# Rows of the first down projection by two engines, urgent splits of v, and two banks of scores in one visit

## The chip, the cores and the metric

The kernel runs on one core of a Trainium2 chip. The metric is the device time of one execution in microseconds (us). The time before the change is the median of three runs. One execution was also taken with the hardware profiler; that is the one whose rows are shown.

## The reference

Sliding-window attention with a distance bias feeds a bilinear feed-forward network (FFN). There are 8 batches, 8 heads, 576 positions, a head dimension of 64; the FFN has 512 inputs, 1536 hidden units and 512 outputs. All is float32.

```python
scores = q @ k.T / sqrt(64) + slopes[h] * (-|i - j|)    # only 0 <= i - j < 128, else -1e9
attn   = softmax(scores)
x      = (attn @ v) laid out as [4608 tokens, 512]
out    = ((x @ w_a) * (x @ w_b)) @ w_out
```

## The kernel before

Every float32 operand of a large product is split into two float16 parts, high and low, after scaling by a power of two, and a product is three matmuls (high-high, high-low, low-high). So most elementwise work is of the form "ACT makes the high part, DVE subtracts it for the low part".

**Attention** goes by pairs of heads, four pairs p = 0 to 3 in a batch. Four PSUM tiles (banks 0 to 3 of `BANKS`) hold a pair's scores. `scores(o, bi)` does the matmuls of one bank (L361 in batch 1, L365 later), then for each of its tiles a bias with minimum on DVE (L369) and an exponential with sum on ACT (L370). `normalize` scales the finished tiles and splits them into `phl` (ACT L382, DVE L383). `transpose_probs` transposes `phl` by DMA into `pT` (L388). `split_v` splits a pair's `v` into `vhl` (ACT L282, DVE L283), with a scale `st.sv` that `v_scale` makes from sums of squares (PE `vtot` L272, then DVE L107, L113, L114). `pv` multiplies `pT` with `vhl` into two PSUM tiles `x_ps` (L482), ACT evicts them into x, in the space of `v`, and takes x's square (`square_x`, L407), which POOL adds to `xq` (L409). After pair 3, `split_x` splits x into `xs` for the FFN, and `hidden_scale` sums the squares over partitions on PE (`n_ps`, L496) and makes the FFN's scale `st.g`. q and k are loaded (SP, L298, L299), split (`split_qk`: ACT L325, DVE L326) and laid out by four DMAs (`qst`, `qkh`, `qkl`, L334 to L337) before a pair's first scores.

**The FFN** of a batch is an up projection (`up_ps`, or `p` and `ch`, L805) and a down projection (`dn_ps`: L787 in batch 0, L901 later). The hidden tiles `rc` come from `new_hidden()`, three buffers; `row()` has two buffers. `bank()` hands out five PSUM tiles in turn for the FFN; three others, of the pool `ps_at`, serve scores, `x_ps` and sums.

**The order.** Batch 0's attention (`first_attention`) comes first, by itself, while the FFN's weights are loaded and converted (generators `up_weights`, `down_weights`: ACT L130, DVE L131 and L133, POOL L135, ACT L141; at the end DVE L222 and the split of the down weights, ACT L230 and DVE L231). Then the FFN of batch b is interleaved with the attention of the batches after it: `attention()` is a generator with places i, one a pair, in sevenths, and `att.along` steps it beside the FFN's groups. A `yield` ends a visit: what stands between two yields goes to TensorE between two pieces of FFN work. In batch 1 and later PE's order is the order of the program; the order of ACT, DVE and POOL, and in batch 0 PE's too, is made by a planner from modelled times and from each instruction's priority, which is its place in the program. SP's order is that of the program up to the end of batch 0's FFN. `tc.high_priority(offset=PRIO)` puts instructions ahead of all that is ready without it. Each engine then takes its instructions strictly in that order. The evictions of the later up and down projections are urgent in this way; those of batch 0's down projection and the splits of `v` are not.

The first down projection, `first_down`, makes four PSUM rows (e = 0 to 3) for each half of the tokens (t = 0, 1) at once, f outermost; ACT writes each to a `row()` buffer (L791) and issues its transfer (L792).

From attention batch 4 on (`two == 2`), banks 0 and 1 of a pair's scores are already done in one visit, and banks 2 and 3 in two visits.

Of the kernel before, what the change touches and what calls it, by code (L numbers as in the profile page):

```python
# [13 lines left out]
BF16 = mybir.dt.bfloat16  # L14
# [3 lines left out]
AF = mybir.ActivationFunctionType  # L18
ALU = mybir.AluOpType
AX = mybir.AxisListType.X  # L20

B, H, S, D = 8, 8, 576, 64
DM, DF = 512, 1536
P = 128
NPAIR = H // 2
# [3 lines left out]
HT = S // 2  # L29
# [13 lines left out]
PRIO = 2000  # L43
# [3 lines left out]
def attention_then_bilinear_ffn(ctx: ExitStack, tc: tile.TileContext, qT, kT, vP, w_a, w_b, w_out, rel, slopes2, outT):  # L47
    nc = tc.nc
    vec, act, pe, pool, sp = nc.vector, nc.scalar, nc.tensor, nc.gpsimd, nc.sync
# [229 lines left out]
    def split_v(st, p):  # L279

        vhl = work.tile([P, 2, VCOLS], F16, tag="vhl", name="vhl", bufs=2)
        act.activation(vhl[:, 0, :], st.v[:, p, :], AF.Copy, scale=st.sv)  # L282
        vec.scalar_tensor_tensor(out=vhl[:, 1, :], in0=st.v[:, p, :], scalar=st.sv, in1=vhl[:, 0, :], op0=ALU.mult, op1=ALU.subtract)  # L283
        return vhl

    def load_plain_qk(b, p):
# [87 lines left out]
    def normalize(o):  # L374

        a, z = o.parts[0][0], o.n

        vec.tensor_scalar(out=o.rin[:, a:z], in0=o.sm[:, a:z], scalar1=1e-9, scalar2=1.0 / PSC, op0=ALU.add, op1=ALU.mult)
        vec.reciprocal(o.rin[:, a:z], o.rin[:, a:z])
        for m, e, pc, w in o.parts:  # L380
            s = o.rin[:, m:m + 1]
            act.activation(phl[:, 0, pc:pc + w], e, AF.Copy, scale=s)  # L382
            vec.scalar_tensor_tensor(out=phl[:, 1, pc:pc + w], in0=e, scalar=s, in1=phl[:, 0, pc:pc + w], op0=ALU.mult, op1=ALU.subtract)  # L383
        o.parts = []
# [12 lines left out]
            act.activation(x[:, c:c + w], ps[:, 0:w], AF.Copy, scale=scale)  # L397
        square_x(p, st, x)

    def square_x(p, st, x, add=True):  # L400

        if p == 0:
            act.activation(st.xq, x, AF.Square, scale=1.02)
            st.squares = [st.xq]
        else:
            sq = work.tile([P, S], BF16, tag="sq", name="sq")
            act.activation(sq, x, AF.Square, scale=1.02)  # L407
            if add:
                pool.tensor_tensor(out=st.xq, in0=st.xq, in1=sq, op=ALU.add)  # L409
            else:  # L410
                st.squares.append(sq)

    B12 = 7

# [69 lines left out]
    def pv(p, st, o, vhl):  # L484
        xp = new_x_ps()
        hi, lo = o.pT[:, 0:NCOL // P, :], o.pT[:, NCOL // P:2 * NCOL // P, :]
        each_pv(xp, (vhl[:, 0, :], vhl[:, 1, :], vhl[:, 0, :]), (hi, hi, lo))
        keep_x(p, st, xp, 1.0 / PSC)
# [16 lines left out]
    def first_attention(weights, rate):  # L505
# [12 lines left out]
        for p in range(NPAIR):  # L518
# [4 lines left out]
            if p == 0:  # L523
# [3 lines left out]
                st = load_v(0)  # L527
# [52 lines left out]
        def pv(p, pt):  # L580


            rin = small.tile([P, QT], F32, tag="rin", name="rin0")
            vec.tensor_scalar(out=rin, in0=sums[p], scalar1=1e-9, scalar2=None, op0=ALU.add)
            vec.reciprocal(rin, rin)
            yield
            rp = [ps_ch.tile([P, 512], F32, tag="ch", name="rin_ps") for _ in range(2)]
            for i in range(QT):
                for e in range(2):
                    r = slice(64 * e, 64 * e + 64)  # L590
                    pe.matmul(rp[i // 8][r, 64 * (i % 8):64 * (i % 8) + 64], rin[r, i:i + 1].to_broadcast([64, 64]), ident[r, r], start=True, stop=True)
            r = first.tile([P, S], F32, tag="rin0", name="rin0", bufs=1)
            x = st.v[:, p, 0:S]
            for n, (c, w) in enumerate(halves_of_x):
                act.copy(r[:, c:c + w], rp[n][:, 0:w])
            xp = [ps_ch.tile([P, 512], F32, tag="ch", name="x_ps") for _ in range(2)]
            each_pv(xp, (st.v[:, p, :],), (pt,))
            yield
            for n, (c, w) in enumerate(halves_of_x):
                vec.scalar_tensor_tensor(out=x[:, c:c + w], in0=xp[n][:, 0:w], scalar=st.sv, in1=r[:, c:c + w], op0=ALU.mult, op1=ALU.mult)  # L600
            yield
            square_x(p, st, x, p < NPAIR - 1)
            yield

        bias(0)
# [33 lines left out]
    def attention():  # L639


        n = NPAIR * (B - 1)
        qks = {}

        def load(i):
            if i < n:

                qks[i] = (load_plain_qk if i < NPAIR else load_qk)(1 + i // NPAIR, i % NPAIR)

        def squares(i):  # L650
            if i >= n:
                return None
            qk = qks.pop(i)
            return qk if i < NPAIR else qk_squares(1 + i // NPAIR, i % NPAIR, qk)

        def split(o):
            if o and o.b > 1:
                split_qk(o)

        def lay_out(o):  # L660
            if o:
                before_scores(o, lay_out_qk(o) if o.b > 1 else -8.0)

        def behind():

            return tc.issue_after(last_read[0].ins) if last_read[0] else ExitStack()

        load(0)
        st, prev = load_v(1), None
        o = squares(0)  # L670
        lay_out(o)
        load(1)
        yield 0
        for i in range(n + 1):
            b, p = 1 + i // NPAIR, i % NPAIR

            two = 2 if o and o.b >= 4 else 1
            for bi in range(two if o else 0):
                scores(o, bi)
            with behind():  # L680
                nxt = squares(i + 1)
            if p == 1 and b > 1:
                st = load_v(b)
            if p == 2:
                v_scale(st)
            yield i + 1 / 7
            if o and two == 1:
                scores(o, 1)

            if p == 2:  # L690

                with tc.issue_after(first_reads[0].ins) if first_reads[0] else ExitStack():
                    late.vhl = split_v(st, late.p)
            elif prev and p != 1:
                prev.vhl = split_v(st, prev.p)
            yield i + 2 / 7
            if p == 2:
                pv(late.p, st, late, late.vhl)
                transpose_probs(prev)
                split(nxt)  # L700
            if o and p != 2:
                with behind():
                    normalize(o)
            if p != 2:
                split(nxt)
            yield i + 3 / 7
            if o:
                scores(o, 2)
            if prev and p not in (1, 2):
                pv(prev.p, st, prev, prev.vhl)  # L710
            yield i + 4 / 7
            if p == 2:
                prev.vhl = split_v(st, prev.p)
                with behind():
                    normalize(o)
            if o:
                scores(o, 3)
            lay_out(nxt)
            load(i + 2)
            if p == 1:  # L720
                v_squares(st, (0, 1))
            if prev and p == 0:
                states[b - 1] = st
                assert started["down"] == b - 2
                for k, _ in enumerate(split_x(st, b - 1 <= 2, b - 1 >= 2)):
                    yield i + (4.2 + 0.2 * k) / 7
            yield i + 5 / 7
            if o:
                with behind():
                    normalize(o)  # L730
            if p == 1:
                v_squares(st, (2, 3))
            yield i + 6 / 7
            if prev and p == 0:
                hidden_scale(st)
            if p == 2:
                pv(prev.p, st, prev, prev.vhl)
            if p == 1:
                late = prev
            elif o:  # L740
                transpose_probs(o)
            prev, o = o, nxt
            yield i + 1
# [4 lines left out]
    def new_hidden():  # L748
        return work.tile([P, 2, HT], F32, tag="rc", name="rc", bufs=3)
# [29 lines left out]
    def first_down(b, oi, h):  # L779

        started["down"] = b
        for t in range(2):
            pss = [bank("dn_ps") for _ in range(NE)]
            for f in range(NF):
                for e in range(NE):
                    for n, (wi, hi) in enumerate(((0, 0), (0, 1), (1, 0))):
                        pe.matmul(pss[e][:, 0:HT], wdn[:, f, wi, e * P:(e + 1) * P], h[:, f, t, hi, :], start=(f == 0 and n == 0), stop=(f == NF - 1 and n == 2))  # L787
                yield
            for e in range(NE):
                o = row()  # L790
                act.activation(o, pss[e][:, 0:HT], AF.Copy, scale=oi)  # L791
                act.dma_start(outT[e * P:(e + 1) * P, b * S + t * HT:b * S + (t + 1) * HT], o)  # L792

    def row():
        return work.tile([P, HT], F32, tag="row", name="row", bufs=2)
# [234 lines left out]
```

## Time and profile before

| | |
|---|---|
| median of three runs | 1038.46 us (1038.11 to 1038.9) |
| the profiled execution | 1035.06 us, its span 1033.3 us |
| granted TensorE clock, mean | 0.98 |
| PE busy | 980.7 us, 95% of the span |
| DVE, ACT, POOL busy | 677.4, 647.5, 315.6 us |

Times in rows are microseconds from the span's start. A row of the order of time has start, duration, engine, line, operation, tiles (out<-in), shapes and count; brackets at its end tell how long the engine was idle before it and what ended that. PE is the matmuls, PEld the weight loads, SPq and ACTq the sequencers that issue transfers. A row of the stretches has the stretch, its length and the busy time of each engine with its count of instructions, then granted clock, share of the DMA engines, GB/s. A row of the transfers has the number issued, KB each, and us from issue to landing. Rough places: batch 0's attention ends at 66, its up projection at 170, its down projection at 219; the FFN of batch 1 begins there; from 570 on each FFN batch takes some 113 us, and the last ends the span.

### The profile page before, as it was taken

The numbers are of one execution on the slowest core, as the hardware profiler recorded it, in microseconds if no ns is written. First come the engines' busy times: TensorE is split into PE (matmuls) and PEld (weight loads), VectorE is DVE, ScalarE is ACT, GpSimd is POOL, SyncE is SP. The second block draws the span as 40 slices with busy tenths as digits, with TensorE's granted clock in tenths as the row PEclk, the third lists the DMA queues.
The fourth block names the chain that finished last, engine by engine and source line by source line (L and its number), as shares of the span: only waits on it lengthen the run. The fifth ranks groups of instructions, "written<-read, shape, count | busy, mean of one in ns | idle before, by whom it ended". The sixth has DMA issues, their size and how long they took to land.

```text
span 1033.3 us, 23882 instructions
## 1 busy us (share of the span) xinstructions
PE 980.7 (95%) x9325; PEld 754.8 (73%) x9325; DVE 677.4 (66%) x1880; ACT 647.5 (63%) x1672; POOL 315.6 (31%) x348
## 2 busy tenths in 40 slices
PE   8789979889999899889999999999999999999998
PEld 6556657667777677667777777777777778787776
DVE  5889988355778656985767667765776576534430
ACT  7977778556667756667666676667666765423321
POOL 3544562000368205880222212321223012221100
PEclk8899989999999999999999999999999999999999
DMA  8335733462543532435434743453624732200001
GB/s 344 125 111 195 251 86 73 100 155 58 123 88 86 145 74 56 87 80 153 88 65 86 184 90 65 88 116 115 124 52 99 173 65 42 48 31 11 1 13 35
DMA packets 148433, 102.83 MB, mean 100 GB/s; under 512 B 120032, under 2 KB 128352, under 8 KB 147296
## 3 DMA queue, kind: packets, MB, share of 16 engines
q1 hardware_dynamic: 138816, 91.77, 35.8%
q10 hardware_dynamic: 9504, 9.54, 2.9%
q8 instruction: 73, 1.20, 0.5%
q14 instruction: 40, 0.33, 0.1%
HBM read 48.33 MB, written 9.44 MB: 56 GB/s over the span
## 4 chain that ended last, share of the span: by engine, by line
PE 58%; DVE 15%; DMA 12%; ACT 7%; issue 3%; POOL 3%; SPq 2%; ACTq 0%; DVEq 0%; POOLq 0%
PE ch L805 16%; PE p L805 13%; PE dn_ps L901 11%; PE up_ps L805 10%; PE x_ps L482 4%; DMA pT<-phl 3%; DVE phl L383 3%; PE sc_ps L365 2%; DVE t L369 2%; ACT phl L382 1%; DMA v<-in_vP 1%; DMA qk<-in_kT 1%; DMA qst<-qkl 1%; DMA qst<-qkh 1%; DMA qkl<-qkl 1%
## 5 line engine op out<-in xcount | busy, mean ns | idle before, releaser
L805 PEld LDWEIGHTS <-wup 128*128 128x128 f16 x4212 | 407.7, 98 | 126.9 <-issue 18.6
L901 PE MATMUL dn_ps<-h,wdn 128*128 128x288 f16 x2016 | 256.8, 287 | 2.5 <-DVE h L799 2.5
L805 PE MATMUL ch<-xs,wup 128*128 128x288 f16 x1584 | 230.0, 287 | 6.7 <-DVE rc L865 4.3
L901 PEld LDWEIGHTS <-wdn 128*128 128x128 f16 x2016 | 193.9, 98 | 56.6 <-issue 3.7
L805 PE MATMUL up_ps<-xs,wup 128*128 128x288 f16 x1440 | 188.1, 289 | 6.0 <-ACT row L791 3.7
L805 PE MATMUL p<-xs,wup 128*128 128x288 f16 x1188 | 178.7, 287 | 0.0
L860 POOL TENSOR_TENSOR rc<-rc,row 128x288 f32<-128x288 f32 x66 | 64.5, 978 | 254.0 <-DVE row L858 235.6
L370 ACT ACTIVATE t<-t,mn 128x192 f32<-128x192 f32 (+2 forms) x252 | 107.4, 428 | 38.6 <-DVE mn L369 36.9
L383 DVE SCALAR_TENSOR_TENSOR phl<-t,rin,phl 128x192 f16<-128x192 f32 (+2 forms) x252 | 103.9, 447 | 34.5 <-ACT phl L382 34.5
L798 ACT CAST h<-rc 128x576 f16<-128x576 f32 x96 | 64.3, 669 | 64.0 <-DVE rc L865 33.1
L382 ACT ACTIVATE phl<-t,rin 128x192 f16<-128x192 f32 (+2 forms) x252 | 88.6, 426 | 19.4 <-DMA pT<-phl 11.4
L799 DVE TENSOR_TENSOR h<-rc,h 128x576 f16<-128x576 f32 x90 | 72.2, 802 | 26.4 <-ACT h L798 25.9
L369 DVE CUSTOM_DVE_ANT_0 t<-sc_ps,bias,neg 128x192 f32<-128x192 f32 (+2 forms) x216 | 74.3, 389 | 13.4 <-PE sc_ps L365 9.6
L842 ACT ACTIVATE row<-ch,g 128x288 f32<-128x288 f32 x66 | 32.9, 498 | 66.0 <-PE ch L805 66.0
L417 DVE TENSOR_TENSOR xs<-v,xs 128x576 f16<-128x576 f32 x51 | 52.5, 1044 | 28.4 <-ACT xs L416 27.9
L135 POOL TENSOR_TENSOR wup<-wup,wdn 128x512 int32<-128x512 int32 x36 | 56.9, 1602 | 33.7 <-issue 5.6
L906 ACT ACTIVATE row<-dn_ps,oi 128x288 f32<-128x288 f32 x56 | 27.7, 495 | 60.4 <-PE dn_ps L901 60.4
L837 DVE TENSOR_TENSOR rc<-p,rc 128x288 f32<-128x288 f32 x66 | 30.0, 454 | 45.5 <-PE p L805 41.5
L409 POOL TENSOR_TENSOR xq<-xq,sq 128x576 bf16<-128x576 bf16 x23 | 34.1, 1481 | 83.7 <-ACT sq L407 83.3
L482 PE MATMUL x_ps<-pT,vhl 128*64 128x128 f16 (+3 forms) x1176 | 47.8, 233 | 5.4 <-DVE vhl L283 2.6
L482 PEld LDWEIGHTS <-vhl 128*64 128x64 f16 (+1 forms) x1176 | 44.1, 112 | 11.2 <-issue 3.9
L365 PEld LDWEIGHTS <-qst 128*64 128x64 f16 x864 | 30.8, 110 | 27.8 <-issue 24.6
(139 smaller groups left out, 1301.1 us busy)
## 6 DMA issues: line engine op xcount, KB each, us to landing
v<-in_vP SPq DMA_DIRECT2D x8, 1280.0 KB, 6.6
out<-row ACTq DMA_DIRECT2D x64, 144.0 KB, 1.8
qk<-in_qT SPq DMA_DIRECT2D x28, 288.0 KB, 3.9
qk<-in_kT SPq DMA_DIRECT2D x28, 288.0 KB, 4.4
wdn<-in_w_a SPq DMA_DIRECT2D x12, 512.0 KB, 4.0
wdn<-in_w_b SPq DMA_DIRECT2D x12, 512.0 KB, 4.9
wdn<-in_w_out SPq DMA_DIRECT2D x12, 512.0 KB, 4.8
qst<-qkh SPq DMA_DIRECT2D x24, 144.0 KB, 2.4
```

The costliest lines, as they stand in the source:

```text
L135: pool.tensor_tensor(out=t[:, m, :], in0=t[:, m, :], in1=low[:, m, :], op=ALU.add)
L369: vec.tensor_tensor_reduce(out=t[:, c:c + w], in0=ps[:, c:c + w], in1=o.bias[:, WIN - w:WIN], scale=-0.125 if o.b == 1 else o.neg, scalar= ...
L370: act.activation(t[:, c:c + w], t[:, c:c + w], AF.Exp, bias=o.mn[:, n:n + 1], scale=-1.0, accum_out=o.sm[:, n:n + 1])
L382: act.activation(phl[:, 0, pc:pc + w], e, AF.Copy, scale=s)
L383: vec.scalar_tensor_tensor(out=phl[:, 1, pc:pc + w], in0=e, scalar=s, in1=phl[:, 0, pc:pc + w], op0=ALU.mult, op1=ALU.subtract)
L417: vec.tensor_tensor(out=xs[:, n, 1, :, :], in0=src, in1=xs[:, n, 0, :, :], op=ALU.subtract)
L482: pe.matmul(xp[oc // 512][64 * h:64 * h + 64, o0:o0 + w], vt[0:rows, c:c + 64], probs(pt, rows, blocks, h), start=(n == 0 and first), stop ...
L798: act.copy(h[:, f, :, 0, :], hid)
L799: eng.tensor_tensor(out=h[:, f, :, 1, :], in0=hid, in1=h[:, f, :, 0, :], op=ALU.subtract)
L805: pe.matmul(ps[:, 0:HT], wup[:, a[0], a[1], wi, k, :], xs[:, b, xi, k, :], start=(first and n == 0), stop=(last and n == len(ks) - 1), ski ...
L860: pool.tensor_tensor(out=x0, in0=x0, in1=mid, op=ALU.mult)
L901: pe.matmul(ps[:, 0:HT], wdn[:, f, wi, e * P:(e + 1) * P], h[:, f, t, hi, :], start=(m == 0 and n == 0), stop=(m == NF - 1 and n == 2))
```

## The change

Four edits.

- `split_v`: its two instructions are urgent until batch 1's x is complete (`states.get(1)`), that is for the four pairs of batch 1.
- `square_x` in batch 0: the square of pair 2 is kept in a tile of its own in the pool `first`, as pair 3's already was in `work`, and goes to `hidden_scale` as one more operand of the sum on PE. Only pair 1's is added by POOL.
- `attention()`: from batch 4 on, for pairs 1 and 3, `scores(o, 3)` follows `scores(o, 2)` (and pair 3's `pv`) in the same visit. Pairs 0 and 2 stay.
- `first_down`: rows 0 and 2 by ACT, 1 and 3 by DVE, all urgent; rows 2 and 3 are written to a tile of `new_hidden()`, not to `row()`. ACT still issues their transfers.

```diff
     def split_v(st, p):
         vhl = work.tile([P, 2, VCOLS], F16, tag="vhl", name="vhl", bufs=2)
-        act.activation(vhl[:, 0, :], st.v[:, p, :], AF.Copy, scale=st.sv)
-        vec.scalar_tensor_tensor(out=vhl[:, 1, :], in0=st.v[:, p, :], scalar=st.sv, in1=vhl[:, 0, :], op0=ALU.mult, op1=ALU.subtract)
+        with tc.high_priority(offset=PRIO) if not states.get(1) else ExitStack():
+          act.activation(vhl[:, 0, :], st.v[:, p, :], AF.Copy, scale=st.sv)
+          vec.scalar_tensor_tensor(out=vhl[:, 1, :], in0=st.v[:, p, :], scalar=st.sv, in1=vhl[:, 0, :], op0=ALU.mult, op1=ALU.subtract)
         return vhl
...
-    def square_x(p, st, x, add=True):
+    def square_x(p, st, x, keep=None):
         if p == 0:
             act.activation(st.xq, x, AF.Square, scale=1.02)
             st.squares = [st.xq]
+        elif keep:
+            sq = keep.tile([P, S], BF16, tag="sq", name="sq")
+            act.activation(sq, x, AF.Square, scale=1.02)
+            st.squares.append(sq)
         else:
             sq = work.tile([P, S], BF16, tag="sq", name="sq")
             act.activation(sq, x, AF.Square, scale=1.02)
-            if add:
-                pool.tensor_tensor(out=st.xq, in0=st.xq, in1=sq, op=ALU.add)
-            else:
-                st.squares.append(sq)
+            pool.tensor_tensor(out=st.xq, in0=st.xq, in1=sq, op=ALU.add)
...
-            square_x(p, st, x, p < NPAIR - 1)
+            square_x(p, st, x, first if p == 2 else work if p == 3 else None)
...
             if prev and p not in (1, 2):
                 pv(prev.p, st, prev, prev.vhl)
+            if two == 2 and p in (1, 3):
+                if p == 2:
+                    with behind():
+                        normalize(o)
+                scores(o, 3)
             yield i + 4 / 7
             if p == 2:
                 prev.vhl = split_v(st, prev.p)
-                with behind():
-                    normalize(o)
-            if o:
+                if two == 1 or p not in (1, 3):
+                    with behind():
+                        normalize(o)
+            if o and (two == 1 or p not in (1, 3)):
                 scores(o, 3)
...
+            more = new_hidden()
             for e in range(NE):
-                o = row()
-                act.activation(o, pss[e][:, 0:HT], AF.Copy, scale=oi)
+                o = row() if e < 2 else more[:, e - 2, :]
+                with tc.high_priority(offset=PRIO):
+                    if e % 2:
+                        vec.tensor_scalar(out=o, in0=pss[e][:, 0:HT], scalar1=oi, scalar2=None, op0=ALU.mult)
+                    else:
+                        act.activation(o, pss[e][:, 0:HT], AF.Copy, scale=oi)
                 act.dma_start(outT[e * P:(e + 1) * P, b * S + t * HT:b * S + (t + 1) * HT], o)
```

## The prediction

> **What bounds the kernel now.** I read the engine totals first, then the sums by stretch, then TensorE's waits, then the order of time inside the stretches that the edits touch.
>
> ```profile
> span 1033.3 us, 23882 instructions
> PE 980.7 (95%) x9325; PEld 754.8 (73%) x9325; DVE 677.4 (66%) x1880; ACT 647.5 (63%) x1672; POOL 315.6 (31%) x348
> ...
> 69.00:170.00 101.00, 90.80 (x789) 66.69 (x788) 92.38 (x201) 81.38 (x190) 47.05 (x37) 0.96 0.50 162
> 170.00:235.00 65.00, 57.40 (x535) 42.54 (x535) 31.01 (x121) 37.07 (x107) 8.07 (x7) 0.95 0.55 129
> 570.00:670.00 100.00, 99.02 (x970) 77.24 (x968) 68.13 (x209) 66.51 (x178) 22.26 (x22) 1.00 0.48 107
> ```
>
> After each stretch stand its length, then PE, PEld, DVE, ACT and POOL busy. From 570 on PE has 1.0 us of idle time in 100: there only less PE work helps. From 170 to 235, where the first down projection runs, PE is idle 7.6 us although DVE is half idle: waits bound it. From 69 to 170 DVE is busy 92.4 of 101: conversion of the weights on DVE, ACT and POOL bounds it, and a PE wait there is not the time by itself.
>
> **Banks 2 and 3 in one visit.** For pairs 1 and 3 of batches 4 to 7, eight visits go:
>
> ```profile
> 585.43 0.27 PE L365 MATMUL sc_ps<-qkh,qst 128*64 128x192 f16 x2
> 585.54 0.25 PE L365 MATMUL sc_ps<-qkl,qst 128*64 128x192 f16 x2
> 585.62 0.25 PE L365 MATMUL sc_ps<-qkh,qst 128*64 128x192 f16 x2
> 585.71 0.25 PE L365 MATMUL sc_ps<-qkl,qst 128*64 128x192 f16 x2
> 585.89 2.38 PE L901 MATMUL dn_ps<-h,wdn 128*128 128x288 f16 x18
> 588.20 0.27 PE L365 MATMUL sc_ps<-qkh,qst 128*64 128x192 f16 x2
> ...
> 588.65 7.53 PE L901 MATMUL dn_ps<-h,wdn 128*128 128x288 f16 x60
> ...
> 597.47 0.22 PE L365 MATMUL sc_ps<-qkl,qst 128*64 128x64 f16 x2 [0.41 <-DMA qkl<-qkl]
> ```
>
> The pitch of a projection's matmul is (7.53 - 0.29) / 59 = 0.123 us. From 585.89 to 588.65 are 2.76: 18 x 0.123 = 2.21, and 0.55 for a visit of 8 matmuls. These stand 0.085 apart in pairs, 4 x 0.085 = 0.34, so a visit costs 0.21 beside its work. Eight make 1.7. But after pair 1's visits PE waits 0.41 for pair 2's `qkl`, whose chain ends on a transfer: what is saved there is waited for. Only pair 3's four count: 4 x 0.21, some 0.9 us. Ends: 1.7, and a loss where bank 3 finds no free PSUM buffer (of three, two hold the product with `v`) or its four DVE and ACT steps, now beside that product's, hold back an eviction: the stretch's other idle time, 1.0 - 0.41 = 0.6, is such a wait at the most, so 4 x 0.6 = 2.4 as an estimate. No transfer, SP or POOL instruction is moved past another.
>
> **First down projection (rows by two engines).** What PE waited for, ACT's order, and the transfers:
>
> ```profile
> 193.66 2.75 PE L787 MATMUL dn_ps<-h,wdn 128*128 128x288 f16 x21 [0.20 <-ACT row L791]
> 199.99 2.32 PE L787 MATMUL dn_ps<-h,wdn 128*128 128x288 f16 x9 [3.21 <-ACT row L791]
> 202.40 1.79 PE L482 MATMUL x_ps<-pT,vhl 128*64 128x128 f16 x32
> 219.58 1.64 PE L805 MATMUL up_ps<-xs,wup 128*128 128x288 f16 x12
> 221.96 3.10 PE L805 MATMUL up_ps<-xs,wup 128*128 128x288 f16 x24 [0.73 <-ACT row L791]
> 230.03 4.77 PE L805 MATMUL up_ps<-xs,wup 128*128 128x288 f16 x24 [2.94 <-ACT row L791]
> ...
> 199.44 0.50 ACT L791 ACTIVATE row<-dn_ps,oi 128x288 f32<-128x288 f32 x1 [3.43 <-DMA out<-row]
> 227.20 0.74 ACT L265 ACTIVATE vsq<-v 128x640 bf16<-128x640 f32 x1 [2.84 <-DMA v<-in_vP]
> 229.50 0.48 ACT L791 ACTIVATE row<-dn_ps,oi 128x288 f32<-128x288 f32 x1
> 231.74 0.49 ACT L791 ACTIVATE row<-dn_ps,oi 128x288 f32<-128x288 f32 x1
> 232.13 0.39 ACT L816 COPY rc<-up_ps 128x288 f32<-128x288 f32 x1
> ```
>
> In the first half, row 2 (of 0 to 3) needs a `row` buffer whose transfer is still out, ACT stands 3.43 us, and PE, out of banks, 0.20 + 3.21 = 3.41. In the second, rows 2 and 3 stand in ACT's queue behind squares of `v` that wait for a load: PE loses 0.73 + 2.94 = 3.67. The edit writes rows 2 and 3 to a buffer of their own, two of the four rows move to DVE, and all are urgent. Both causes go. No row shows this operation on DVE; at ACT's 0.49 us, or at twice that, four of them lie in DVE's 34 idle us of 65 and cost nothing; without that cover a half would end two rows, 1 us, later. ACT still issues all transfers, so ACT stands until DVE's row is done, under 0.5 us.
>
> What is late next? In the first half, the product with `v` at 202.40 would come 3.41 earlier, at 198.99, but it needs the transposed probabilities:
>
> ```profile
> 191.78 4.91 SPq L388 DMA_TRANSPOSE pT<-phl  x1
> pT<-phl SPq DMA_TRANSPOSE x1, 9.4
> ...
> pT<-phl SPq DMA_TRANSPOSE x1, 6.7
> ```
>
> (The 9.4 is of this transfer, the 6.7 of the one issued at 255.84, with no row beside it.) It lands at 191.78 + 9.4 = 201.2, so PE waits 2.2 there and 1.2 of the 3.41 is left. If it took 6.7, all 3.41 would be. If two more rows beside it cost as much again as the two did (2.7), it lands at 203.9 and the half loses 1.5. I take 1.2, the row itself; ends -1.5 and 3.41. The Trainium skill ("DMA: Bandwidth & Descriptors", Issuing engines are not separate DMA queues) says that transfers of all issuing engines interleave on the same 16 DMA engines; 9.4 against 6.7 agrees, and by it four rows at once give the 1.5 us loss, not the gain.
>
> In the second half, PE runs on until the eighth group of the next up projection needs the bank of the third, which ACT reads at 232.13. A group is 12 matmuls of 0.123 us, 1.47; seven of them and two visits of 0.55 from 219.58 end at 231.0. ACT reads the bank 0.48 + 0.49 earlier, as two rows left its queue: done at 231.5. So 0.5 of 3.67 stays; I take 3.2, ends 0 (the load of `v` still holds ACT to 227.20) and 3.67. Together 4.4, from -1.5 to 7.1.
>
> **Norm of batch 0.** Pair 2's square is kept, not added by POOL:
>
> ```profile
> 64.74 1.73 POOL L409 TENSOR_TENSOR xq<-xq,sq 128x576 bf16<-128x576 bf16 x1
> 66.52 0.53 PE L496 MATMUL n_ps<-xq,ones 128*128 128x512 bf16 x2 [2.03 <-POOL xq L409]
> 71.97 0.42 PE L496 MATMUL n_ps<-sq,ones 128*128 128x512 bf16 x2
> 72.23 2.98 PE L805 MATMUL up_ps<-xs,wup 128*128 128x288 f16 x23
> ```
>
> The add stands behind POOL's weight work and PE waits 2.03 for it. Instead PE sums one more operand: two more matmuls, 72.23 - 71.97 = 0.26. Gain 2.03 - 0.26 = 1.75. Batch 1's first scores and the weight steps that PE feeds come after it in PE's order and move with it. Ends: 0 (pair 3's square, not pair 2's, ends last) and 2.03.
>
> **Urgent splits of v, batch 1.**
>
> ```profile
> 128.55 0.25 PE L272 MATMUL vtot<-vc,ones 128*128 128x1 bf16 x4
> 139.23 0.14 DVE L114 TENSOR_SCALAR sv<-r 128x1 int32<-128x1 int32 x1
> 141.19 0.28 PE L482 MATMUL x_ps<-pT,vhl 128*64 128x128 f16 x4 [2.24 <-ACT vhl L282]
> 141.34 1.89 DVE L133 SCALAR_TENSOR_TENSOR wup<-wdn,wup 128x1024 int32<-128x1024 int32 x1
> 143.15 3.73 DVE L283 SCALAR_TENSOR_TENSOR vhl<-v,sv,vhl 128x640 f16<-128x640 f32 x2
> 145.10 2.75 PE L482 MATMUL x_ps<-pT,vhl 128*64 128x128 f16 x38 [2.64 <-DVE vhl L283]
> 140.41 7.62 POOL L135 TENSOR_TENSOR wup<-wup,wdn 128x512 int32<-128x512 int32 x4
> 149.39 0.16 DVE L222 TENSOR_REDUCE wo<-wos 128x1 f32<-128x6 f32 x1 [2.08 <-ACT wdn L141]
> 164.58 4.57 PE L805 MATMUL up_ps<-xs,wup 128*128 128x288 f16 x36 [0.53 <-ACT rc L758]
> ```
>
> PE waits 2.24 + 2.64 = 4.88 for `vhl`. Urgent splits shorten that, but the two of 3.73 us then go ahead of L133 at 141.34, the last step of the weights on DVE; POOL's L135 waits for it, then ACT's square, L222, the conversion of the down weights, and PE stands at 164.05 for ACT behind that conversion. What PE gains at 141, it would wait out there, unless the conversion comes earlier too. So gain 0; ends +4.88 and -3.73 (all of the two splits put ahead). I take 0, as the wait at 164.58 shows that PE is already ahead of ACT. If that cover were gone, 4.88 is the worth. Nothing is issued on SP for these steps. The Trainium skill ("SBUF — State Buffer", Who interferes with whom) says that a DVE instruction with two SBUF inputs contends with GpSimd's reads; the pair beside L135 agrees (1.87 us each). By it a split moved within POOL's stretch gets no cheaper, which leaves the zero.
>
> **The sum.** ACT's, DVE's and, in batch 0, PE's order come from a planner; I hold its order as it was but for the instructions named. 4.4 + 1.75 + 0 + 0.9 = 7.05 us. The profiled execution took 1035.06 us (span 1033.3, 1.8 around it), 3.4 under the median of the runs, 1038.46. 1035.06 - 7.05 = 1028.0 on its scale; on the median's, 1031.4, which I predict.
>
> **Rivals.**
> 1. The stretch from 170 to 235 is set by its transfers (transpose 9.4, rows, load of `v`), so the rows give 0, and the visits 0: only the norm's 1.75 is left, 1036.7. For it: ACT's 3.43 and 2.84 are waits for transfers. Against: PE's waits all name the rows. Chance 0.20; it lies at the border of a change.
> 2. The conversion moves with PE, and the urgent splits pay their 4.88: 1038.46 - 7.05 - 4.88 = 1026.5. For it: the square before L222 stands in ACT's queue behind evictions that wait for PE. Against: POOL's L135 ends at 148.03 anyway. Chance 0.15.
> 3. Slower: the planner puts an urgent split into ACT's order before the scale `sv` exists on the chip. ACT takes its queue in order, and `sv` comes 139.37 - 128.80 = 10.6 us after the matmul that it needs, because DVE is behind. All of ACT's weight work would stand for up to that: 1038.46 - 7.05 + 10.6 = 1042.0. It decides from 7.05 us of such standing. For it: DVE's share of 92 in 101. Against: the trace of before shows no such standing, ACT reached the split after `sv`. Chance 0.10.
>
> **How the numbers follow.** The forecast has 0.55, with its own range of 1027 to 1036 (ends of the first half and of the visits). A measurement of this kernel can tell some 0.2%, 2.1 us: faster is under 1036.4, slower over 1040.5. Faster: 0.55, rival 2's 0.15 and 0.08 of rival 1, 0.78; same 0.12; slower 0.10. The range reaches from rival 2 with a little of its margin, 1025.5, to rival 1, 1037.0, and leaves out 0.2.
>
> **What would show it.** After: no wait of PE on L791 in the first down projection, rows under two engines, some 2 us of wait for `pT` instead; no wait on L409 at 66; the waits on `vhl` shorter, but a longer one near 164; pair 3's banks 2 and 3 on both sides of one product with `v`; pair 2's `qkl` wait grown from 0.41 to some 0.6. Wrong: a wait near 128 to 140 on ACT's split, or a later L222.

## The result and the profile after

The changed kernel takes 1024.86 us, median of four runs (1024.22 to 1026.58), against 1038.28 for the kernel before beside it: a ratio of 0.9879, 95% interval 0.9863 to 0.9894, so 11 to 14 us less. The forecast of 1031.4 had the sign and about half of the size (7.05); its range ended at 1025.5, 0.6 above the time. On the scale of the 1038.46 from which it was worked out, the ratio gives 1025.9, just inside.

The page's engine totals of the kernel after:

```profile
span 1022.4 us, 23891 instructions
PE 973.8 (95%) x9327; PEld 752.8 (74%) x9327; DVE 683.7 (67%) x1884; ACT 644.3 (63%) x1668; POOL 310.2 (30%) x347
```

The sums of the two stretches that the prediction weighed, of the kernel after:

```profile
69.00:170.00 101.00, 89.39 (x803) 66.46 (x800) 93.64 (x193) 77.88 (x176) 43.38 (x36) 0.99 0.50 162
170.00:235.00 65.00, 62.35 (x604) 47.30 (x602) 38.95 (x139) 41.30 (x120) 9.01 (x8) 1.00 0.62 142
```

DVE still bounds the first of them. From 170 to 235 PE is now idle 2.65 us, not 7.6, and in the same row the granted clock (third number from the end) rose from 0.95 to 1.00. PE's busy time fell by 6.9 us over the span, though it has two matmuls more to do: the same work ran at a higher clock. The prediction's sum has no term for that.

The order of time around the first down projection, of the kernel after:

```profile
196.17 1.63 PE L485 MATMUL x_ps<-pT,vhl 128*64 128x128 f16 x42
197.73 3.11 PE L796 MATMUL dn_ps<-h,wdn 128*128 128x288 f16 x24
...
214.86 3.10 PE L820 MATMUL up_ps<-xs,wup 128*128 128x288 f16 x24 [0.33 <-ACT row L806]
...
225.39 6.04 PE L820 MATMUL up_ps<-xs,wup 128*128 128x288 f16 x48 [0.43 <-ACT rc L831]
233.32 3.10 PE L820 MATMUL up_ps<-xs,wup 128*128 128x288 f16 x24 [1.89 <-ACT rc L831]
```

The stall between the halves (3.21 on a row) is gone, and the product with `v` does not wait for the transposed probabilities, which the prediction said it would for 2.2. In the second half 0.33 is left of the 3.67 for the rows, and PE waits 0.43 and 1.89 for ACT's copy of `up_ps` instead. And 24 matmuls take 3.10 us, where the row at 230.03 of the kernel before had taken 4.77. Ahead of the copy for which PE waits 1.89 (ACT, 232.89), ACT stands for a load:

```profile
230.86 1.16 ACT L309 ACTIVATE qkl<-qk 128x1152 bf16<-128x1152 f32 x1 [2.33 <-DMA qk<-in_kT]
```

The next section shows the same thing where it cost more; this one is still there.

Counted at the same matmul of the FFN in both traces, the kernel after is 0.9 us ahead at the start of the first down projection, 6.7 ahead from its second half on, 9.2 at the second down projection, 6.2 at the third and 10.9 at the end. The 3.0 go mostly near 343: PE waits 3.43 + 0.66 for `qkh` and `qkl` there, where the kernel before had 2.67 + 0.43, and a stretch of half clock (granted clock 0.50) follows, which the profiled execution of before escaped.

### The profile page after: what moved, and what is told of

Its sections match the earlier page's. It is cut to its first block, busy times and chain, and to the rows that moved or that the text cites. A ratio compares the mean times of both kernels' runs of the same rounds, so it can differ in the third digit from the quotient of the medians.

```text
span 1022.4 us, 23891 instructions
## 1 busy us (share of the span) xinstructions
PE 973.8 (95%) x9327; PEld 752.8 (74%) x9327; DVE 683.7 (67%) x1884; ACT 644.3 (63%) x1668; POOL 310.2 (30%) x347
## 4 chain that ended last, share of the span: by engine, by line
PE 61%; DVE 10%; DMA 7%; ACT 6%; issue 3%; POOL 2%; SPq 1%; ACTq 0%; DVEq 0%; POOLq 0%
PE dn_ps L916 17%; PE ch L820 16%; PE p L820 12%; PE up_ps L820 8%; PE x_ps L485 3%; PE sc_ps L366 3%; DVE phl L384 2%; DMA v<-in_vP 2%; PE dn_ps L796 2%; DMA qk<-in_kT 2%; DMA pT<-phl 2%; ACT t L371 1%; DVE t L370 1%; ACT phl L383 1%; ACT qkl L309 1%
## 5 line engine op out<-in xcount | busy, mean ns | idle before, releaser
L820 PE MATMUL up_ps<-xs,wup 128*128 128x288 f16 x1440 | 185.2, 287 | 8.2 <-DVE rc L769 4.6
L135 POOL TENSOR_TENSOR wup<-wup,wdn 128x512 int32<-128x512 int32 x36 | 54.6, 1538 | 44.5 <-DVE wup L133 9.7
L348 POOL TENSOR_SCALAR bias<-rel_sb,ninv,sl_sb 128x192 f32<-128x192 f32 x24 | 17.3, 722 | 118.7 <-DVE mn L370 118.7
L239 POOL TENSOR_TENSOR wa<-wup 128x512 f32<-128x512 f16 x24 | 30.6, 1277 | 62.5 <-DVE phl L384 61.8
L880 DVE SCALAR_TENSOR_TENSOR rc<-rc,g,ch 128x288 f32<-128x288 f32 x66 | 33.6, 510 | 23.2 <-PE ch L820 23.2
```

The lines of the kernel that those rows point to most:

```text
L135: pool.tensor_tensor(out=t[:, m, :], in0=t[:, m, :], in1=low[:, m, :], op=ALU.add)
L820: pe.matmul(ps[:, 0:HT], wup[:, a[0], a[1], wi, k, :], xs[:, b, xi, k, :], start=(first and n == 0), stop=(last and n == len(ks) - 1), ski ...
L880: vec.scalar_tensor_tensor(out=x1, in0=x1, scalar=st.g, in1=ch, op0=ALU.mult, op1=ALU.mult)
```

## What the first down projection owes to ScalarE's order

The time here came from something that the prediction held fixed. ACT's order in the kernel before, from 182 on:

```profile
187.19 1.16 ACT L308 ACTIVATE qkl<-qk 128x1152 bf16<-128x1152 f32 x1 [4.36 <-DMA qk<-in_kT]
...
189.78 1.49 ACT L382 ACTIVATE phl<-t,rin 128x192 f16<-128x192 f32 x4 [0.45 <-DVE rin L379]
```

The square of the next `q` and `k` (L308) stands ahead of pair 3's last exponentials and normalizing, and ACT stands 4.36 us for its load. The transposition can only be issued behind that, at 191.78. The same place after (lines are 1 higher), ACT, then SP's sequencer, then the transfers with their us from issue to landing:

```profile
183.07 1.49 ACT L383 ACTIVATE phl<-t,rin 128x192 f16<-128x192 f32 x4 [0.45 <-DVE rin L380]
187.94 1.16 ACT L309 ACTIVATE qkl<-qk 128x1152 bf16<-128x1152 f32 x1 [3.39 <-PE sc_ps L366]
```

```profile
185.07 5.45 SPq L389 DMA_TRANSPOSE pT<-phl  x1
```

```profile
pT<-phl SPq DMA_TRANSPOSE x1, 8.1
```

The planner now puts L309 behind the normalizing; the transposition goes out 6.7 us earlier and lands at 193.2, not 201.2. None of the four edits names these instructions. Which edit moved them, and what that alone is worth, the experiments show.

## Each edit alone

Ratios are to the kernel before; 0.001 is 1.04 us.

**Rows alone** (`first_down` of the diff above, nothing else).

```diff
+            more = new_hidden()
...
+                o = row() if e < 2 else more[:, e - 2, :]
+                with tc.high_priority(offset=PRIO):
+                    if e % 2:
+                        vec.tensor_scalar(out=o, in0=pss[e][:, 0:HT], scalar1=oi, ...)
```

> The kernel before with the first down projection's rows alone changed. Theory (waits and the clock after them): the trace of after has 4.4 us less PE idle time between 190 and 240 and none of the two stretches of half clock (3.41 us each) that stood there before, some 3 us more; so 7 to 8 us faster than before, near 1031, and no half clock at 200 and 231. Rival (idle time alone): 4.4 us faster, near 1034.

Measured: 0.9999 (0.9978 to 1.0020), no difference to within some 2.2 us; neither 4.4 nor 7 to 8 came. PE's rows at the end of the first half, then the transposition among the transfers:

```profile
202.15 2.91 PE L482 MATMUL x_ps<-pT,vhl 128*64 128x128 f16 x42 [3.84 <-DMA pT<-phl]
204.99 4.30 PE L787 MATMUL dn_ps<-h,wdn 128*128 128x288 f16 x24
```

```profile
pT<-phl SPq DMA_TRANSPOSE x1, 9.9
```

The wait for the row is gone and one of 3.84 for `pT` stands in its place, followed by half clock (4.30 for 24 matmuls). This execution is 0.6 behind that of before where the projection starts; PE begins the product with `v` 0.25 ahead, so 0.8 is won up to there. Behind it 2.0 are lost, as half clock now lasts 6.8 us, not 3.4. From there to 235, in the second half, PE goes from 1.75 behind to 3.6 ahead. It then waits 2.0 at 239 for a copy of ACT, which had stood 2.45 for a load (L308) ahead of that copy; half clock follows again, and PE is 0.2 behind the kernel before.

**Norm alone** (`square_x` with `keep`).

```diff
-            square_x(p, st, x, p < NPAIR - 1)
+            square_x(p, st, x, first if p == 2 else work if p == 3 else None)
```

> The kernel before with batch 0's norm alone changed. Prediction: 1.75 us faster. Theory from the trace of after: the planner moves the sums and batch 1's first scores ahead, PE then waits for DVE instead, and the weights' conversion sets the stage's end, so within 1 us of before. The start of the first down projection (169.9 before) tells.

Measured: 0.9943 (0.9929 to 0.9957), 6 us less, more than either expectation. But not at the norm: this profile starts its first up projection 3.6 us later than that of before (1.6 of them stood at 46, ahead of anything that the edit touches), and is still 1.3 behind where the first down projection starts. It gains 4.8 us between the halves of that projection, without the rows' edit: the transposition is issued at 186.46 and lands at 194.24, and PE no longer waits there. The edit made the planner put L308 behind the normalizing. It moved other instructions of ACT and DVE too, from 57 us on; what those are worth by themselves was not measured.

**Splits alone** (urgent `split_v`).

```diff
+        with tc.high_priority(offset=PRIO) if not states.get(1) else ExitStack():
```

> The kernel before with the urgent splits of v alone. Prediction: 0, ends 4.9 us faster and 3.7 slower. Theory from the trace of after: PE's waits on the splits shrink but others on DVE grow, first down projection at most 1 us earlier, no more than 1 us of time. Rival: 3 to 5 us faster (PE's waits go for good).

Measured: 0.9995 (0.9980 to 1.0011), the zero of the prediction, but not for its reason. PE's waits from 115 to 165 in this kernel:

```profile
PE x_ps L483 <- DVE vhl L284: 2.8, 1, 2.8
PE x_ps L483 <- ACT vhl L283: 2.3, 1, 2.3
```

They are as long as before (2.64 and 2.24). On DVE the two splits still stand behind L133 (143.71, before 143.15); up to 169 the edit moved only two of ACT's splits (near 150 and 166), by one place each. So the question of where the saved 4.88 would be waited out was never put.

**Visits alone** (banks 2 and 3 together for pairs 1 and 3).

```diff
+            if two == 2 and p in (1, 3):
+                scores(o, 3)
             yield i + 4 / 7
```

> The kernel before with banks 2 and 3 in one visit alone. Prediction: 0.9 us faster, pair 2's wait for qkl grown to 0.6. Theory from the trace of after: pair 2's waits (0.41 to 0.72, four of them) go too, because the scores of pair 1 free the buffer qst earlier and its transfers start earlier; 1.7 + 2.0 less 0.9 of a new wait, so 2.5 to 3 us faster.

Measured: 0.9961 (0.9943 to 0.9979), 4 us less, over four times the term of 0.9.

## ScalarE's order by itself, and the rows with it

On ACT the square of `q` and `k` and the reading of its sum change their place, on DVE the instruction that uses the sum (L311) follows; the order of PE, POOL and SP is that of before. None of the four edits is in:

```diff
-            act.activation(phl[:, 0, pc:pc + w], e, AF.Copy, scale=s)
+            normed[0] = act.activation(phl[:, 0, pc:pc + w], e, AF.Copy, scale=s)
...
-            with behind():
+            with tc.issue_after(normed[0].ins) if i == 4 else behind():
                 nxt = squares(i + 1)
```

> The kernel before with ScalarE's order alone changed: the square of the next q and k (L308), at which it stood 4.27 us for their load at 187.11, is put behind the exponentials and normalizing of pair 3 of batch 1 (L370 x2, L382 x4). Nothing of the four edits is in it. Theory (the norm edit paid by this order): the transposed probabilities are issued near 186 and land near 195 instead of 201.2, the stall of 3.2 us between the two halves of the first down projection goes or shrinks below 1, its half clock with it; 4 to 6 us less, as the norm edit alone had. Rival (the norm edit paid by its own sums, 2 us, and the rest is chance of the clock): no change within 1 us. Second rival: the square of q and k is now late for the next batch, and 2 us or more come back behind 240.

Measured: 0.9956 (0.9942 to 0.9971), 4.6 us less (3 to 6). ACT's rows in this kernel, then PE's at both stalls:

```profile
184.86 1.49 ACT L382 ACTIVATE phl<-t,rin 128x192 f16<-128x192 f32 x4 [0.75 <-DVE rin L379]
187.77 1.16 ACT L308 ACTIVATE qkl<-qk 128x1152 bf16<-128x1152 f32 x1 [1.41 <-DMA qk<-in_kT]
```

```profile
198.04 1.70 PE L482 MATMUL x_ps<-pT,vhl 128*64 128x128 f16 x42
199.67 3.11 PE L787 MATMUL dn_ps<-h,wdn 128*128 128x288 f16 x24
...
225.01 5.92 PE L805 MATMUL up_ps<-xs,wup 128*128 128x288 f16 x24 [3.22 <-ACT row L791]
```

The first stall is gone with the rows' code untouched, and ACT waits only 1.41 for the load. Most of the norm edit's 6 us is this order. Why the row's wait went too: the rows' transfers now go out with the transposition already running for 5 us, and ACT's wait for the third row's buffer was 0.66, not 3.43. The second stall stays, 3.22, with half clock behind it.

The trace is 4.8 us ahead of before's after the first stall and level with it at the end. Of this, 3.4 go between 306 and 357, where this execution has 6.8 us of half clock (from 350.3) and that of before none. The profiled execution of before was also 3.5 under its median beside this kernel, so the 4.6 rest on the runs and not on these two traces.

**Rows with that order:**

> The same order of ScalarE together with the rows of the first down projection by two engines, still without norm, splits and visits. Theory (rows alone gave nothing because the transposed probabilities were late, then at the second half the gain fell to a later wait at half clock): with them early both stalls go, 7 to 9 us less than before, and 2 to 4 less than the order alone. Rival (the rows' second half is given back at 239 in any order): the same time as the order alone within 1 us.

Measured: 0.9940 (0.9924 to 0.9957). In the trace both stalls go (0.31 and 1.74 of waits for ACT's copy of `up_ps` are left, as after) and it is 4.6 us ahead of the order alone at the second down projection. The times say 1.7 +- 2.3 us less than the order alone: the expected 2 to 4 and zero both lie within. (The profiled execution was the fastest of this kernel's, that of the order alone its slowest.) So the rows pay behind the order if they pay at all, and how much stays open.

**The change without the norm edit:**

```diff
-            square_x(p, st, x, first if p == 2 else work if p == 3 else None)
+            square_x(p, st, x, p < NPAIR - 1)
```

> The changed kernel without the norm edit (rows, splits and visits stay). Theory (the norm edit gave its 6 us through ScalarE's order at 183 to 190, which the other three need too): ScalarE stands at L308 for the load again, and the time is 6 to 9 us above the changed kernel's 1024.9, near 1031 to 1034. The prediction's term (the wait of 2.03 us at the norm, 1.75 on the path): 1.75 above, near 1026.6.

Measured: 0.9932 (0.9915 to 0.9950), 1031.7 us: 5 to 7 us of the gain are lost with an edit that the prediction put at 1.75. PE's costliest wait from 180 to 245 in this kernel (engine and line that waited, what for, us, times, longest):

```profile
PE x_ps L483 <- DMA pT<-phl: 4.2, 2, 3.4
```

As in the rows alone, the product with `v` waits for a late transposition. At the norm itself the edit moved a wait rather than removing it. PE's order there after:

```profile
62.69 0.41 PE L499 MATMUL n_ps<-sq,ones 128*128 128x512 bf16 x2
66.24 0.61 PE L156 MATMUL wn_ps<-wdn,ones 128*128 128x256 bf16 x4 [3.14 <-DVE mn L370]
```

The sums and batch 1's first scores come earlier, and the weights' sums now wait 3.14 for a PSUM buffer that DVE frees (2.03 for POOL before).

## The visits: pair 1 or pair 3

```diff
+            if two == 2 and p in (1,):      # in the second kernel: (3,)
+                scores(o, 3)
             yield i + 4 / 7
...
-            if o:
+            if o and (two == 1 or p not in (1,)):
                 scores(o, 3)
```

> The kernel before, with the visit made one for pair 1 alone from the fourth batch on; pair 3 stays in two visits, nothing else of the change is in. On SyncE this puts the two transfers of qst ahead of the next loads of q and k, four times. Theory (the visits paid because the loads of qkl no longer stand behind other loads on SyncE): the four waits of 0.41 to 0.72 us for qkl at pair 2 are gone and the next passes start without one; 2 to 3 us less than before, more than half of the 4 that both pairs' visits gave. Rival (what pair 1 saves is waited for by pair 2, as the prediction said): four waits for qkl of 0.4 to 0.9 stay and the time is that of before within 0.5 us.

> The kernel before, with the visit made one for pair 3 alone; pair 1 stays in two visits. On SyncE the load of the next k comes ahead of one transfer, four times. The prediction's term: 4 times 0.21 us, 0.9 us less, with the waits for qkl at pair 2 as before. Theory from the traces: 0 to 1 us less, the waits for qkl stay at 0.41 to 0.72. Rival (pair 3 gave most of the 4 us): 2 us less or more.

Measured: pair 1 alone 0.9964 (0.9949 to 0.9980), 3.7 us less; pair 3 alone 0.9983 (0.9968 to 0.9999), 0.1 to 3.3 us less (1.8 by the ratio, 1.0 by the medians): the term of 0.9 lies within, and so do the rival's 2 us. PE's waits from 480 to 1015, pair 1 alone and then pair 3 alone:

```profile
PE ch L807 <- DVE rc L867: 2.3, 4, 0.6
PE ch L807 <- ACT row L844: 0.9, 2, 0.5
```

```profile
PE ch L807 <- DVE rc L867: 2.3, 4, 0.6
PE sc_ps L365 <- DMA qkl<-qkl: 2.0, 4, 1.0
PE sc_ps L365 <- DMA qkh<-qkh: 0.9, 2, 0.5
```

With pair 1's visits gone, the waits for `qkh` and `qkl` are gone: the four for `qkl` made 2.0 us in the kernel before too. The cause stands in SP's queue, here of the kernel before and then of the kernel after, between pair 1 and pair 2 of the same batch:

```profile
588.67 0.67 SPq L298 DMA_DIRECT2D qk<-in_qT  x1
589.39 0.64 SPq L299 DMA_DIRECT2D qk<-in_kT  x1
590.12 0.56 SPq L334 DMA_DIRECT2D qst<-qkh  x1
590.73 0.59 SPq L335 DMA_DIRECT2D qst<-qkl  x1
```

```profile
578.45 0.47 SPq L335 DMA_DIRECT2D qst<-qkh  x1
579.90 0.46 SPq L336 DMA_DIRECT2D qst<-qkl  x1
580.45 0.66 SPq L299 DMA_DIRECT2D qk<-in_qT  x1
581.52 0.47 SPq L337 DMA_DIRECT2D qkh<-qkh  x1
582.20 0.46 SPq L338 DMA_DIRECT2D qkl<-qkl  x1
582.71 0.65 SPq L300 DMA_DIRECT2D qk<-in_kT  x1
```

`lay_out` and `load` stand behind bank 3's scores in the step. With bank 3 in the earlier visit, the transfers into `qst`, which pair 2's scores need, go ahead of both loads of the pair after next, and those of `qkh` and `qkl` ahead of the second. Before, `qkl` was issued at 594.88 and landed at 597.43, where PE stood for it; after, it is issued at 582.20 and lands at 585.61, and PE asks for it at 587.84. With pair 1 alone, DVE and POOL keep the order of before and ACT swaps one pair of exponentials a batch; SP's order and the visits are what differs. No run moved these transfers alone, so what they are worth is read from the traces: four visits of 0.21 and waits of 2.4 make 3.2, near the 3.7.

## The splits within the change

The change with ordinary splits (the two lines of `split_v` as before):

> The changed kernel with the splits of v not urgent any more (rows, norm and visits stay). Theory (the splits alone gave nothing, but in the change they halve two waits of 2.24 and 2.64 us around 140 into ones below 2.0, and so spare a stretch of half clock of 6.83 us there): the half clock near 142 is back and the time is 1 to 3 us above the changed kernel's 1024.9. Rival (the splits give nothing in any company, the prediction's 0): within 1 us of 1024.9, with or without the half clock.

Measured: 0.9888 (0.9870 to 0.9906) against the change's 0.9879, 0.9 +- 2.5 us. Both theories lie within, and that of a half clock near 142 fails on the trace: this kernel has its stretches nearest to it at 134.40 and 154.88, and no wait of PE on `vhl` at all, where the changed kernel has one of 1.5. So it was not the urgency that shortened these waits: with the norm edit alone and ordinary splits, one of 1.5 is left too. The splits' worth stays under what these runs can tell.

## The half clock

The granted clock in the traces is 1.00 or 0.50, and it changes only at places 3.41 us apart: all starts of 0.50 in one trace lie on one grid, whose offset differs from execution to execution. Four pairs of neighbouring stretches of that grid, the kernel before (stretch, length, busy PE, PEld, DVE, ACT, POOL, then the clock):

```profile
196.38:199.79 3.41, 0.40 (x6) 0.27 (x6) 0.00 (x0) 0.35 (x1) 0.00 (x0) 1.00 0.87 187
199.79:203.20 3.41, 3.21 (x26) 2.10 (x27) 0.67 (x3) 2.64 (x7) 0.00 (x0) 0.50 0.26 89
227.10:230.51 3.41, 0.48 (x4) 0.38 (x4) 2.20 (x8) 3.31 (x9) 0.00 (x0) 1.00 0.02 8
230.51:233.92 3.41, 3.41 (x17) 2.16 (x15) 2.11 (x4) 3.41 (x11) 0.00 (x0) 0.50 0.28 91
349.98:353.39 3.41, 1.42 (x12) 0.89 (x10) 1.97 (x7) 3.41 (x11) 0.00 (x0) 1.00 0.57 178
353.39:356.80 3.41, 2.29 (x29) 1.77 (x30) 1.51 (x10) 2.33 (x9) 0.00 (x0) 1.00 0.35 93
418.24:421.65 3.41, 1.36 (x16) 0.87 (x15) 3.41 (x6) 2.44 (x6) 3.33 (x5) 1.00 0.31 82
421.65:425.06 3.41, 3.41 (x15) 2.15 (x16) 3.29 (x8) 1.36 (x6) 3.41 (x3) 0.50 0.83 182
```

PE idle 3.01, 2.93 and 2.05 us: the next stretch runs at 0.50. Idle 1.99: it doesn't. Over the 14 profiles of this study, from 55 to 1015 us, a full-clock stretch with 2.04 us of idle PE or more was followed by half clock 52 times in 52, one with less than 1.7 not once in over 3700, and between them it went both ways. A half-clock stretch was followed by another if PE was idle in it for 0.55 us or more (22 of 23), else by full clock (71 of 71). These bounds are read off the same profiles; two kernels further down put them to the test. Each costs up to 1.7 us of matmul work. From 50 to 1015 us the profile before has 23.9 us of half clock, that after 10.2, so up to 6.8 of the 10.9 us between the spans. How a wait falls on the grid decides: the wait of 2.08 at 460.53 brought half clock before; its like at 454.08 after, also 2.08 but across a border, did not.

**Matmuls put into a wait.** The kernel before, with 24 matmuls of no use to the result ahead of the group that waits at 227:

```diff
+        if st is states.get(1) and f == 1:
+            fill = ps_at.tile([P, 512], F32, tag="at", name="fill_ps")
+            for n in range(24):
+                pe.matmul(fill[:, 0:HT], wup[:, f, 0, 0, 0, :], xs[:, 0, 0, 0, :], start=True, stop=True)
```

> The kernel before with 24 matmuls more on TensorE, of no use to the result, ahead of the up projection's group that waits 2.94 us at 227. Theory (half clock follows a wait of 2 to 3 us): they fill the wait, the 24 matmuls behind it take 3.1 us instead of 4.77 and no granted clock of 0.50 stands near 231; the time is 1 to 2 us less, though more work is done. Rival (the half clock there has another cause, or falls on the same place anyway): the 24 behind take 4.7 again, the time is the same or longer by up to 3.1.

PE's rows at that place:

```profile
229.82 3.10 PE L813 MATMUL fill_ps<-xs,wup 128*128 128x288 f16 x24
232.76 1.63 PE L805 MATMUL up_ps<-xs,wup 128*128 128x288 f16 x12
234.93 1.63 PE L805 MATMUL up_ps<-xs,wup 128*128 128x288 f16 x12 [0.54 <-ACT row L791]
```

In place the theory holds: the 24 behind take 1.63 twice, no stretch there is at 0.50, and from 219 to 238 this kernel is 1.6 us faster with 24 matmuls more. The time isn't: 1.0022 (1.0007 to 1.0038), 2 us longer. The edit also moved some of ACT's and DVE's instructions after it; whether the loss is theirs wasn't settled.

The same on the change, where only PE's order differs:

```diff
+        for n in range(44 if (o.b, o.p, bi) == (3, 2, 0) else 0):
+            pe.matmul(ps[:, 0:P], ones16, ones16, start=True, stop=True)
```

> The changed kernel with 44 small matmuls (ones by ones, 128x128, of no use to the result) on TensorE ahead of the scores that wait 3.40 us for their transposed keys at 342.87; the order of no other engine differs. Theory (a stretch of 3.41 us in which TensorE idles over 2.0 us is followed by 3.41 us at half clock): they leave under 2.0 us of idle there, no granted clock of 0.50 stands between 343 and 353, and the time is 1 to 2 us less than the changed kernel's 1024.9, though more work is done. Rival (half clock follows the wait for the transfer whatever TensorE does, or the small matmuls don't count as work): the half clock stays, the time is the same or up to 1 us longer.

PE's rows at that place, then the sums of two neighbouring stretches of the grid:

```profile
342.27 2.62 PE L757 MATMUL sc_ps<-ones 128*128 128x128 bf16 x44
346.47 0.22 PE L366 MATMUL sc_ps<-qkh,qst 128*64 128x64 f16 x2 [1.58 <-DMA qkh<-qkh]
```

```profile
343.55:346.97 3.42, 1.56 (x26) 1.30 (x23) 0.97 (x4) 2.10 (x5) 0.00 (x0) 1.00 0.58 152
346.97:350.38 3.41, 2.96 (x23) 1.90 (x24) 1.28 (x9) 1.68 (x7) 0.00 (x0) 0.50 0.00 0
```

Not as the theory had it: the wait fell from 3.43 to 1.58 and the idle time to 1.86, and half clock came all the same. Ratio 0.9878 (0.9858 to 0.9897), no gain over the change. 1.86 lies in the mixed band; whether small matmuls count for less, or the border is just there, can't be told from this.

## Why the prediction came out as it did, step by step

- **The sum's assumption failed first**: "I hold its order as it was but for the instructions named". The norm edit changed the planner's order of ACT 120 us later. That order alone is worth 4.6 us. So that the sign and half of the size came out is in good part luck: the rows' 4.4 paid nothing by themselves, and the norm edit's 1.75 came as 6 us through the order and not through its wait.
- **Rows, 4.4.** Alone, the first half won 0.8 of the 1.2 up to the product with `v`, as the forecast had it: PE waits for the transposition. That took 9.9 us beside four rows' transfers, not the 12.1 of the -1.5 end; the half loses 1.2 all the same, but to half clock behind the wait, which the sum doesn't have. The Trainium skill ("DMA: Bandwidth & Descriptors", Issuing engines are not separate DMA queues) says that transfers started by different engines run on the same 16 DMA engines and interleave; 9.9 beside four rows, 9.4 beside two and 6.7 beside none agree. The second half won 5.4 (the wait of 3.67 and the half clock behind it) and gave 3.8 back at 239. On DVE a row took 0.5 us, as supposed. In the change both stalls go, since `pT` came 8 us earlier. So rival 1 was right on the rows alone, in part by its mechanism, and on nothing else.
- **Norm, 1.75.** The wait on POOL went, as written, and one of 3.14 on DVE took its place. Where the first down projection starts, the kernel after is 0.9 ahead and the norm alone 1.3 behind; in the time the edit has 5 to 7 us, most of it from the order.
- **Splits, 0.** Right in number, by luck: the term weighed two splits going ahead of L133 against PE's shorter waits, and alone neither came. The waits on `vhl` shortened with the norm edit's order. The longer wait expected near 164 did not come. Rivals 2 and 3 did not happen.
- **Visits, 0.9.** Pair 3's four: within what was measured. Pair 1's: "what is saved there is waited for" and "No transfer, SP or POOL instruction is moved past another" were wrong; transfers move past loads on SP, the waits for `qkl` go instead of growing to 0.6, and pair 1 gives 3.7 (2.1 to 5.3), not 0.
- **The missing term**: half clock behind a wait. Two rows quoted in the prediction carry it, 4.77 for x24 at 230.03 beside 3.10 for the same x24 at 221.96, and 2.32 for x9 at 199.99. A stall of 3 us ending there cost 1.1 to 1.7 more than its own length.

By the ratios, norm alone (5.9), visits alone (4.0) and the rows' 1.7 behind the order make 11.6 of the change's 12.6; each has 1.5 to 2.3 us on either side, so the sum shows only that nothing large is missing.

## What to carry to other kernels

Where a planner orders the queues, compare each queue's order in the two builds before any term is put at zero: here the largest single part that was shown came from an instruction that no edit names, moved from in front of work that the next stage needed. An instruction that waits for a load should not stand ahead of one whose result starts a long transfer; that single change of order, on the kernel before, gave a third of what the whole change gave. The kernel after still has such a place, at 230.86. Price a stall with the work behind it: compare the duration of equal groups of matmuls before and behind the wait.

## What the runs showed of the hardware

I had not expected that half clock follows so sharp a count: some 2 us of idle TensorE in a stretch of 3.41 us on a fixed grid, and back to full as soon as a stretch has under 0.55. As the grid's offset differs each time, a wait such as that of 2.08 can cost half clock in one execution and not in another. The kernel before went from 1033.5 to 1041.5 us in 22 runs, which the half clock can explain in part; that it explains all of it wasn't shown.
